# Float16 halves for every key block, rows of maxima by a transposition, and a written order of the heads' events

## The chip, the cores and the metric

The kernel runs on one core of a Trainium2 chip. The metric is device microseconds of one execution of the whole program: attention over 16 heads, a dense two-layer mixture, and a routed mixture of eight experts. The kernel before takes 713.42 us (median of three runs, 712.31 to 713.80).

In what follows PE is TensorE, ACT is ScalarE, DVE is VectorE, POOL is GpSimd and SP is SyncE. SBUF is the on-chip memory that all engines read, PSUM the one that PE writes its products to.

## The reference, cut to what matters

Attention compares only queries and keys whose random projections have the same six sign bits; all others are masked.

```python
q_bits = (einsum('bhsd,dk->bhsk', q, proj) > 0); k_bits = ...   # 6 bits a token
mask   = q_bucket[..., :, None] == k_bucket[..., None, :]
scores = where(mask, q @ k.T / sqrt(D), -1e9)                   # B=2, H=8, S=768, D=64
attn   = exp(scores - max(scores)); attn /= sum(attn) + 1e-9
x      = (attn @ v) as (1536, 512)
x      = (s * relu(x @ w_in)**2 + b) @ w_out                    # first mixture, d_ff 2048
e      = argmax(x @ w_gate + modality_bias[id])                 # second mixture, 8 experts
out    = gate * (relu(x @ w1[e]) @ w2[e])
```

A query whose bucket holds no key at all has a row of equal scores, so its result is the mean of all values. The kernel handles this with flags: a flag of such a query multiplies the sum of all values.

## The kernel before, in words

**Heads.** Two heads that share a batch entry make a pair (NP = 8 pairs). A head has 768 queries and 768 keys, in NB = 6 blocks of 128. Per pair, q and k come by transfer, are transposed on PE (`trans`, line 219), split into a high and a low part by ACT (line 227) and DVE (line 229), and copied into operand tiles Q1, K1, Q2, K2 by transfers on SP (`asm`); `bits` (line 286) makes the bucket bits.

**Maxima.** For each block of queries `maxp` multiplies Q1 by K1 (line 425) and DVE takes the row maximum from PSUM (line 428). When a head's six blocks are through, `mops` (lines 436 to 441) makes on DVE the shifted maximum in two bfloat16 parts, and the flags. `mrow` turns these columns into rows on PE with an identity: heads 0 to 3 by six products of a padded tile MD (line 447) and one of MP (line 448), after which ACT writes two rows of Q1 directly (line 450) and the flags (line 452); heads 4 to 15 by one product of MP (line 461), an ACT copy (line 464), an ACT copy of the flags NM (line 465) and two transfers on SP into Q1 (line 468). So the maximum is subtracted within the score product itself.

**Scores and values.** `st` computes a block of keys against all queries (line 477, four products into two PSUM banks), ACT takes the exponent into e (line 480), ACT rounds e to float16 eh (line 487), and POOL makes the rest el = e - eh (line 490). There are five buffers each for eh and el, four for e, and three score tiles of two PSUM banks. `avs` multiplies e by the values in two groups of three queries: with halves, three stationary eh blocks with two products each (high and low values VX) and three el blocks with one (line 501, `mm`). The constant NH = 5 says that only the first five blocks of a head are so treated, four for pair 7; the other blocks are multiplied in float32 (tile VW, no eh and no el). The last block's `avs` also multiplies the flags NM by the value sums VS. `fin` normalizes on DVE.

**Value sums and scales.** The values are scaled by a power of two taken from their mean size (`vabs`, `vred`, `vscale0` to `vscale2`), for three groups of pairs: 0, 1 to 3, 4 to 7. `vsums` (lines 388 to 394) makes the sums of all values of each head in parts on 12 partitions, in vb. `vsel` (line 399) spreads them for one pair on POOL into VS. `vxs` (line 405) scales the values, `vx` rounds them (line 412) and `vxl` makes the low part (line 416).

**Order.** Each engine takes its instructions in the order in which the program issues them. `program` lists the steps of all these functions as events; the part of a function up to a `yield` is one event. An event stands at 10 g + priority, with g the number of the key block in time (6 h + j); a step is named like `st:3,2/1`. The table MOVED gives 80 or so events another place. The events are sorted and issued. Work of the first mixture (`w_a`, `w_b`, `lead_k`, at g from 71 on) stands among the last heads. Behind the heads `Moe.program` issues the two mixtures, each in an order of its own.

Of the kernel before, what the change touches and what calls it, by code (L numbers as in the profile page):

```python
# [18 lines left out]
S = 768  # L19
# [9 lines left out]
NH = 5  # L29
XN = [[f"x{g}{i}" for i in "hl"] for g in range(3)]  # L30
MOVED = {
# [16 lines left out]
}  # L48
# [12 lines left out]
class Attn:  # L61
    def __init__(self, ctx, natctx, hlctx, qkctx, qkctx2, tc, psS, psA, ident, identb, q, k, v, proj, xt, x1, x2):
# [31 lines left out]
        self.MP = [c.tile([128, 128], BF16, name=f"MP{i}") for i in range(2)]  # L94
        self.MD = [t[1 + i][:, 1408:1408 + HALF].bitcast(BF16).rearrange("p (j q) -> p j q", j=NB) for i in range(2)]
        self.WD = [w[:, 128 * i:128 * i + 128] for i in range(2)]
        self.VX = [c.tile([128, 2, NH, 130], F16, name=f"VX{i}") for i in range(2)]
        self.VW = [c.tile([128, 2, 1 + i, 66], F32, name=f"VW{i}") for i in range(2)]
        self.VS = [c.tile([128, NB, 2, 66], F16, name=f"VS{i}") for i in range(2)]
        self.NM = [c.tile([128, 128], F16, name=f"NM{i}") for i in range(3)]  # L100
# [54 lines left out]
    def setup2b(self):  # L155
        nc = self.nc
        for i in range(2):
            nc.gpsimd.memset(self.MP[i], 0.0)
            nc.gpsimd.memset(self.MD[i], 0.0)
            nc.gpsimd.memset(self.VX[i][:, :, :, 64:65], 1.0)  # L160
            nc.gpsimd.memset(self.VW[i][:, :, :, 64:65], 1.0)
            nc.gpsimd.memset(self.vb[i][:, :, 65:66], 0.0)
            nc.gpsimd.memset(self.VS[i], 0.0)
        for i in range(3):
            nc.gpsimd.memset(self.NM[i], 0.0)
# [18 lines left out]
    def vmask(self):  # L184
        nc = self.nc
        idv = self.ident[0:12, 0:12].rearrange("p (c j) -> p c j", c=2)
        nc.vector.tensor_reduce(out=self.msk[:, 0:2], in_=idv, axis=AX.X, op=ALU.add, negate=True)
        nc.vector.tensor_tensor(out=self.msk[:, 2:8], in0=idv[:, 0], in1=idv[:, 1], op=ALU.add)
# [157 lines left out]
    def nh(self, p):  # L346
        return NH - (p == self.NP - 1)

# [25 lines left out]
    def vscale2(self, i):  # L374
        o = 256 * (i == 0)
        ps = self.vtile(i)[:, o:o + 3]
        self.nc.tensor.matmul(out=ps, lhsT=self.one[0:1], rhs=self.vsr[0:1, 0:3])
        yield
        self.nc.vector.tensor_copy(self.sc[i], ps)

    def vsums(self, lo, hi):
        nc, V = self.nc, self.nc.vector
        a, n = lo // 4, 2 * (hi - lo)
        hs = slice(2 * lo % 8, 2 * lo % 8 + n)
        cs = slice(hs.start * D, hs.stop * D)
        r0, p1, vb, src = self.vr0[:, cs], self.vp1[:, cs], self.vb[a], self.vtile(self.group(lo))[0:12, cs]
        sc = self.sc[self.group(lo)][0:12, 2:3]
# [3 lines left out]
        V.scalar_tensor_tensor(out=vb[:, hs, 0:D], in0=p1.rearrange("p (h d) -> p h d", h=n), scalar=self.msk[:, 1:2],  # L391
                               in1=r0.rearrange("p (h d) -> p h d", h=n), op0=ALU.mult, op1=ALU.add)
        V.tensor_scalar(out=vb[:, hs, D:D + 1], in0=self.msk[:, 0:1].unsqueeze(1).to_broadcast([12, n, 1]),
                        scalar1=-S * CSH * 2.0 ** -15, scalar2=None, op0=ALU.mult)

    def vsel(self, p):
        sh = [12, NB, 132]
        h = 2 * p % 8
        self.nc.gpsimd.tensor_tensor(out=self.VS[p % 2][0:12].rearrange("p j h d -> p j (h d)"),
                                     in0=self.vb[p // 4][:, h:h + 2].rearrange("p h d -> p (h d)").unsqueeze(1).to_broadcast(sh),  # L400
                                     in1=self.msk[:, 2:8].unsqueeze(2).to_broadcast(sh), op=ALU.mult)

    def vxs(self, p):
        vn = self.vn[p]
        self.nc.gpsimd.tensor_scalar(out=vn, in0=vn, scalar1=self.sc[self.group(p)][:, 0:1], scalar2=1.0, op0=ALU.mult, op1=ALU.mult)
        yield
        n = self.nh(p)
        self.nc.gpsimd.tensor_copy(self.VW[p % 2][:, :, 0:NB - n, 0:D], vn[:, :, n:])

    def vx(self, p):  # L410
        n = self.nh(p)
        self.nc.scalar.activation(out=self.VX[p % 2][:, :, 0:n, 0:D], in_=self.vn[p][:, :, 0:n], func=ACTF.Copy)

    def vxl(self, p, hh):
# [1304 lines left out]
```

## Time and profile before

| | |
|---|---|
| median of three runs | 713.42 us (712.31 to 713.80) |
| the profiled execution | 712.21 us, span 710.3 us |
| PE, busy | 677.8 us (95%) |
| PE's weight loads, busy | 595.4 us (84%) |
| DVE, busy | 423.6 us (60%) |
| ACT, busy | 368.8 us (52%) |
| POOL, busy | 238.5 us (34%) |
| mean granted TensorE clock | 0.992 |

The span runs from the first to the last instruction. The heads take about the first 268 us, the first mixture stands up to about 500 us, the routed one behind it. Busy shares are over the whole span, so ACT and POOL, which do most of their work among the heads, look emptier than they are there. A row in the next section that begins with a time gives the start in us, the length in us, the engine, the line of the kernel, the operation, its tile and shape and the number of merged instructions. Since products are pipelined, the step from one start to the next tells what a group takes; its own length holds the latency of the last one too.

### The profile page before, as it was taken

To read this page: it belongs to the slowest core of one execution; us is meant where nothing else is said; L and a number is where in the kernel's file an instruction comes from. 1 tells how busy PE (TensorE), PEld (TensorE's weight loads), DVE (VectorE), ACT (ScalarE), POOL (GpSimd) and SP (SyncE) were. 2 spreads that over 40 slices of the span, in tenths; PEclk is the share of its full clock that TensorE was granted. 3 is DMA by queue.
4 is the path that set the end of the run, shared out by engine and by line. 5 is a ranking of instruction groups with operands and counts; after the bars stand their busy time and mean duration, and the time that the engine had idled before them with its cause. 6 is when DMAs were issued, how large, how long until landed. Compare 5 with 4: busy or idle time off the path is not lost.

```text
span 710.3 us, 12827 instructions
## 1 busy us (share of the span) xinstructions
PE 677.8 (95%) x5003; PEld 595.4 (84%) x5003; DVE 423.6 (60%) x813; ACT 368.8 (52%) x580; POOL 238.5 (34%) x264
## 2 busy tenths in 40 slices
PE   9898999999989899999999999999999999999992
PEld 6677889988977788788888888888889999999992
DVE  5857766767667768888883432245663675645311
ACT  5666887787768775556542232232452263444411
POOL 8586887787767730000000000200110504040102
PEclk9999999999999999999999999999999999999997
DMA  9589345635571222344310000011431356354101
GB/s 194 140 209 211 72 105 119 152 87 122 122 173 55 61 90 90 119 139 128 118 60 0 16 31 15 1 45 50 138 113 45 115 186 211 119 168 147 45 16 47
DMA packets 52998, 72.33 MB, mean 102 GB/s; under 512 B 30320, under 2 KB 30832, under 8 KB 52928
## 3 DMA queue, kind: packets, MB, share of 16 engines
q1 hardware_dynamic: 49808, 62.24, 32.8%
q0 software_dynamic: 2960, 9.18, 4.0%
q8 instruction: 41, 0.67, 0.4%
q14 instruction: 29, 0.24, 0.1%
q10 hardware_dynamic: 160, 0.00, 0.0%
HBM read 46.31 MB, written 6.42 MB: 74 GB/s over the span
## 4 chain that ended last, share of the span: by engine, by line
PE 74%; ACT 8%; issue 7%; DVE 6%; POOL 2%; DMA 1%; SPq 0%; POOLq 0%; DVEq 0%; ACTq 0%
PE Y L1028 17%; PE H L970 16%; PE H L1345 8%; PE Y L1365 7%; PE Sst L477 7%; PE av L501 6%; ACT e L480 4%; PE Smaxp L425 3%; PE Sbits L286 2%; PE mlr L1058 1%; PE Strans L219 1%; ACT eh L487 1%; PE wps L269 1%; PE mxt L1332 1%; POOL out_dram L1419 1%
## 5 line engine op out<-in xcount | busy, mean ns | idle before, releaser
L490 POOL TENSOR_TENSOR el<-e,eh 128x768 f16<-128x768 f32 x78 | 128.5, 1651 | 55.4 <-ACT eh L487 40.9
L1028 PE MATMUL Y<-gh,W 128*128 128x512 f32 x384 | 128.8, 393 | 0.5 <-DVE sv L1038 0.5
L428 DVE TENSOR_REDUCE mx<-Smaxp 128x1 f32<-128x768 f32 x96 | 91.5, 983 | 42.9 <-PE Smaxp L425 42.8
L480 ACT ACTIVATE e<-Sst 128x768 f32<-128x768 f32 x96 | 77.3, 805 | 42.2 <-PE Sst L477 37.8
L477 PE MATMUL Sst<-Q,K 128*128 128x384 f32 x384 | 91.5, 360 | 6.7 <-DVE mx L428 2.9
L1028 PEld LDWEIGHTS Y<-gh,W 128*128 128x128 f32 x384 | 72.1, 188 | 15.6 <-DVE sv L1038 0.9
L1365 PE MATMUL Y<-hh,W 128*128 128x400 f32 x256 | 79.0, 353 | 0.0
L1028 PE MATMUL Y<-gl,W 128*128 128x512 f32 x192 | 74.8, 390 | 0.0
L983 DVE SCALAR_TENSOR_TENSOR r<-r,sb 128x512 f32<-128x512 f32 x46 | 35.8, 778 | 62.5 <-ACT r L982 62.3
L477 PEld LDWEIGHTS Sst<-Q,K 128*128 128x128 f32 x384 | 63.3, 190 | 11.1 <-ACT e L480 3.8
L487 ACT ACTIVATE eh<-e 128x768 f16<-128x768 f32 x78 | 65.8, 844 | 2.4
L982 ACT ACTIVATE r<-H 128x512 f32<-128x512 f32 x44 | 26.3, 597 | 78.1 <-PE H L970 78.1
L956 POOL IOTA ev<- 128x96 f32 x1 | 0.3, 299 | 190.5 <-PE H L970 190.5
L990 ACT ACTIVATE gh<-r,sb 128x512 fp32r<-128x512 f32 x46 | 33.2, 725 | 52.9 <-PE Y L1028 52.4
L425 PE MATMUL Smaxp<-K,Q 96*128 96x384 f32 x192 | 50.7, 350 | 5.6 <-ACT e L480 2.4
L991 DVE SCALAR_TENSOR_TENSOR gl<-r,sb,gh 128x512 fp32r<-128x512 f32 x46 | 34.4, 749 | 33.9 <-ACT gh L990 33.7
L501 PE MATMUL av<-VX,eh 128*128 128x65 f16 (+1 forms) x936 | 49.5, 194 | 0.0
L1252 DVE TENSOR_TENSOR W<-st,W 128x1024 fp32r<-128x1024 f32 x32 | 38.9, 1223 | 17.0 <-ACT W L1251 17.0
L501 PEld LDWEIGHTS <-eh 128*128 128x128 f16 x936 | 38.2, 98 | 12.9 <-issue 12.3
L1365 PEld LDWEIGHTS Y<-hh,W 128*128 128x128 f32 x256 | 47.6, 188 | 0.0
L1352 ACT ACTIVATE hh<-H 128x400 fp32r<-128x400 f32 x32 | 16.0, 501 | 55.1 <-PE Y L1365 46.1
L970 PE MATMUL H<-x1h,W 128*128 128x512 f32 x128 | 44.1, 396 | 0.0
(372 smaller groups left out, 1466.4 us busy)
## 6 DMA issues: line engine op xcount, KB each, us to landing
st<-in_moe_w_dram SPq DMA_DIRECT2D x32, 512.0 KB
sw<-in_moe_w_in_dram SPq DMA_DIRECT2D x16, 512.0 KB
sw<-in_moe_w_out_dram SPq DMA_DIRECT2D x16, 512.0 KB
Q<-qh SPq DMA_DIRECT2D x30, 192.0 KB
K<-kh SPq DMA_DIRECT2D x30, 192.0 KB
nq<-in_q_dram SPq DMA_DIRECT2D x16, 192.0 KB
nk<-in_k_dram SPq DMA_DIRECT2D x16, 192.0 KB
yd<-row SPq DMA_DIRECT2D x12, 256.0 KB
```

The lines of the kernel that those rows point to most:

```text
L425: nc.tensor.matmul(out=ps[:, a, 0:HALF], lhsT=self.Q1[i][0:96, j * 128:j * 128 + 128], rhs=self.K1[i][0:96, a * HALF:a * HALF + HALF])
L428: nc.vector.tensor_reduce(out=self.mx[h][:, j:j + 1], in_=ps[:, :, 0:HALF], axis=AX.XY, op=ALU.max)
L477: nc.tensor.matmul(out=ps[:, a, 0:HALF], lhsT=K[:, c], rhs=Q[:, a * HALF:a * HALF + HALF], start=(n == 0), stop=(n == 1))
L480: nc.scalar.activation(out=h2(e), in_=ps[:, :, 0:HALF], func=ACTF.Exp, scale=0.125)
L487: nc.scalar.activation(out=eh, in_=e, func=ACTF.Copy)
L490: nc.gpsimd.tensor_tensor(out=el, in0=e, in1=eh, op=ALU.subtract)
L501: mm = lambda q, n, e, v, start=False, stop=False: nc.tensor.matmul(out=av[:, q, 0:n], lhsT=e, rhs=v, start=start, stop=stop, skip_group_c ...
L970: self.nc.tensor.matmul(out=ps, lhsT=w[:, k, fs], rhs=x[:, k], start=(k == 0 and n == 0), stop=(k == 3 and n == 2))
L1028: nc.tensor.matmul(out=self.yp[d], lhsT=w[:, i, ds], rhs=x, start=(fc in (0, FA) and n == 0), stop=(fc in (FA - 1, 15) and n == 2))
L1252: nc.vector.tensor_tensor(out=lo[:, o], in0=d["st"], in1=f(hi[:, o]), op=ALU.subtract)
L1345: nc.tensor.matmul(out=ps, lhsT=w, rhs=xx[:, kd, 0:C], start=(n == 0), stop=(n == 11))
L1365: nc.tensor.matmul(out=self.yp[d][:, 0:C], lhsT=w, rhs=xx, start=(fc == 0 and n == 0), stop=(fc == 7 and n == 2))
```

## The change: what it does

- NH goes: all six blocks of every head are split into eh and el; VW and the float32 form of `avs` are gone, and VX holds six blocks.
- `mops` becomes two reductions: the maximum against a constant column, and a sum that gives each maximum twice, plainly and shifted. Only head 0 still uses MD. `mrow` of all other heads transposes these 12 columns in one float32 product. ACT copies the rows rounded, DVE makes the difference and (`flags`) the flags, straight from PSUM, and the two transfers on SP take every second row.
- `vsums` has one ACT copy instead of two; the count column of vb is written once at the start, by POOL. `vsel` is replaced by `vstore`: six small transfers on SP per group of pairs spread the sums into one tile VS for eight heads.
- MOVED is built from a list RUNS that places nearly every event of the heads, some 900, in runs of names between two positions. Counts of loads, score products, maxima and value products are as before.

```diff
-NH = 5
-MOVED = {
...
+RUNS = (
...
+    (60, 61, "st:0,4/2 vred:3/1 vabs:4/0 maxp:2,1/0 avs:0,2,1/0 vsums:0,1/1 avs:0,3,0/0 maxp:2,3/1 maxp:2,1/1 avs:0,3,1/0 mrow:1/3 "
+             "load_v:5/0 asm:1,k,(1,)/2 st:0,4/3 maxp:2,2/0"),
...
+    (560, 561, "bits:6/0 st:9,0/2 vstore:4,8/0 st:8,5/3 avs:8,2,0/0 fin:7/0 bits:6/1 st:9,1/2 maxp:11,2/0 vx:5/0 maxp:11,2/1"),
...
+MOVED = {n: lo + (hi - lo) * (i + 1) / (len(s.split()) + 1) for lo, hi, s in RUNS for i, n in enumerate(s.split())}
...
     def vsums(self, lo, hi):
...
-        nc.scalar.activation(out=r0, in_=src, func=ACTF.Copy, scale=sc)
-        nc.scalar.activation(out=p1, in_=src, func=ACTF.Copy, scale=sc)
+        nc.scalar.activation(out=vl, in_=src, func=ACTF.Copy, scale=self.msc[i])
         yield
...
-    def vsel(self, p):
...
+    def vstore(self, lo, hi):
+        hs = slice(2 * lo % 8, 2 * lo % 8 + 2 * (hi - lo))
+        for q in range(NB):
+            self.nc.sync.dma_start(out=self.VS[2 * q:2 * q + 2, q, hs], in_=self.vb[2 * q:2 * q + 2, hs])
...
     def mops(self, h):
...
+        V.tensor_reduce(out=mc[:, :, 0], in_=self.mx2[h % 3], axis=AX.X, op=ALU.max)
+        mx = self.mx[h] = self.sm.tile([128, NB, 2], F32, tag="mc", name="mc")
+        V.tensor_reduce(out=mx, in_=mc.unsqueeze(2).to_broadcast([128, NB, 2, 2]), axis=AX.X, op=ALU.add)
...
+    def flags(self, h, rows):
+        self.nc.vector.tensor_scalar(out=self.NM[h % 3], in0=rows, scalar1=-0.5 * PEN, scalar2=2.0 ** 15, op0=ALU.is_le, op1=ALU.mult)
 
     def mrow(self, h):
-        if h < 4:
+        if h == 0:
             yield from self.mrow0(h)
             return
...
-        nc.tensor.matmul(out=ps[:, 0:128], lhsT=MP, rhs=self.identb)
+        nc.tensor.matmul(out=ps, lhsT=self.mx.pop(h).rearrange("p j r -> p (j r)"), rhs=self.ident, is_transpose=True)
         yield
...
+        hl = [self.sm.tile([12, 128], F32R, tag=f"m{c}", name=f"m{c}", bufs=1) for c in range(2)]
+        nc.scalar.activation(out=hl[0], in_=ps, func=ACTF.Copy)
+        yield
+        nc.vector.tensor_tensor(out=hl[1], in0=ps, in1=f(hl[0]), op=ALU.subtract)
+        self.flags(h, ps)
         yield
...
     def st(self, h, j):
...
-        if j >= self.nh(h // 2):
-            self.E[h, j] = e
-            return
         yield
...
     def avs(self, h, j, t):
...
-        if j >= self.nh(p):
-            e = self.E[h, j]
-            for q in qs:
-                mm(q, 65, e[:, c(q)], self.VW[p % 2][:, hh, j - self.nh(p), 0:65])
-        else:
...
```

## Rows read from the trace of the kernel before

**Rows 1.** Stretches: from:to, length, busy us (instructions) by engine, clock, DMA share, GB/s.

```profile
20.00:80.00 60.00, 53.16 (x537) 44.74 (x535) 42.96 (x73) 43.33 (x66) 45.13 (x45) 0.97 0.72 163
80.00:180.00 100.00, 98.86 (x1165) 90.95 (x1160) 69.77 (x124) 79.88 (x117) 77.03 (x61) 1.00 0.53 117
180.00:260.00 80.00, 72.25 (x821) 63.24 (x820) 55.58 (x94) 61.16 (x92) 55.58 (x45) 1.00 0.38 98
268.00:680.00 412.00, 410.15 (x2224) 359.81 (x2224) 234.99 (x480) 164.56 (x271) 39.68 (x69) 1.00 0.28 91
```

**Rows 2.** Waits of PE: who waited for whom, total us, times, longest.

```profile
PE Sst L477 <- DVE mx L428: 2.9, 2, 2.4
...
PE Sst L477 <- ACT NM L465: 1.5, 1, 1.5
```

**Rows 3.** PE in order of time around the last block of a head and the next head.

```profile
151.28 0.78 PE L501 MATMUL av<-VW,e 128*128 128x65 f32 x6
151.89 0.25 PE L501 MATMUL av<-VS,NM 128*128 128x65 f16 x3
151.98 0.86 PE L501 MATMUL av<-VW,e 128*128 128x65 f32 x6
152.68 0.26 PE L501 MATMUL av<-VS,NM 128*128 128x65 f16 x3
...
153.91 0.36 PE L501 MATMUL av<-VX,eh 128*128 128x65 f16 x6
...
154.19 0.35 PE L501 MATMUL av<-VX,eh 128*128 128x65 f16 x6
...
154.47 0.22 PE L461 MATMUL Smrow<-identb,MP 128*128 128x128 bf16 x1
154.67 0.96 PE L477 MATMUL Sst<-Q,K 128*128 128x384 f32 x4
...
156.38 0.94 PE L477 MATMUL Sst<-Q,K 128*128 128x384 f32 x4
```

**Rows 4.** PE: the rows of maxima of head 2, and float32 transpositions elsewhere.

```profile
56.70 0.50 PE L447 MATMUL Smrow<-identb,tx0l 128*128 128x128 bf16 x6
57.04 0.22 PE L448 MATMUL Smrow<-identb,MP 128*128 128x128 bf16 x1
...
L365 PE MATMUL vps<-iw,vr 128*1 128x128 f32 x2 | 0.5, 272 | 0.0
```

**Rows 5.** ACT by line and shape: busy us, mean ns, idle before.

```profile
L480 ACT ACTIVATE e<-Sst 128x768 f32<-128x768 f32 x96 | 77.3, 805 | 42.2 <-PE Sst L477 37.8 <-PE Smaxp L425 2.3 <-POOL el L490 1.1
L487 ACT ACTIVATE eh<-e 128x768 f16<-128x768 f32 x78 | 65.8, 844 | 2.4
L450 ACT ACTIVATE Q<-Smrow 2x768 fp32r<-2x768 f32 x4 | 3.2, 804 | 5.5 <-PE Smrow L448 5.4
...
L465 ACT ACTIVATE NM<-Smrow 12x128 f16<-12x128 f32 x9 | 2.4, 266 | 0.2
```

**Rows 6.** POOL by line and shape, in the same form.

```profile
L490 POOL TENSOR_TENSOR el<-e,eh 128x768 f16<-128x768 f32 x78 | 128.5, 1651 | 55.4 <-ACT eh L487 40.9 <-issue 7.5 <-POOL el L490 2.7
...
L399 POOL TENSOR_TENSOR VS<-vb,msk 12x792 f16<-12x792 f16 x8 | 12.5, 1556 | 0.0
```

**Rows 7.** DVE by line and shape: the small operations of `mops`.

```profile
L436 DVE TENSOR_SCALAR mc<-mx 128x6 f32<-128x6 f32 x16 | 6.7, 417 | 0.1
L437 DVE TENSOR_SCALAR MP<-mx 128x12 bf16<-128x12 f32 x16 | 5.7, 357 | 0.0
...
L440 DVE CAST MP<-mc 128x6 bf16<-128x6 f32 x12 | 2.0, 170 | 0.0
```

**Rows 8.** POOL and DVE in order of time, from 59 to 63 us.

```profile
59.43 2.87 DVE L393 TENSOR_SCALAR vb<-msk 12x6 f16<-12x6 f32 x1
...
61.50 0.77 POOL L416 TENSOR_TENSOR VX<-tx0h,VX 128x320 f16<-128x320 f32 x1
```

**Rows 9.** The chain that ended last, in order of time: start, us, what.

```profile
38.75 2.33 DMA K<-aux
```

More of the change, by code (lines that the diff above doesn't have):

```diff
@@ L93, in __init__ @@
         self.Q1, self.K1, self.Q2, self.K2 = zip(*sets)
-        self.MP = [c.tile([128, 128], BF16, name=f"MP{i}") for i in range(2)]
-        self.MD = [t[1 + i][:, 1408:1408 + HALF].bitcast(BF16).rearrange("p (j q) -> p j q", j=NB) for i in range(2)]
+        self.MD = t[1][:, 1408:1408 + HALF].bitcast(BF16).rearrange("p (j q) -> p j q", j=NB)
         self.WD = [w[:, 128 * i:128 * i + 128] for i in range(2)]
[L97 to L100, printed above, removed]
+        self.VX = [c.tile([128, 2, NB, 130], F16, name=f"VX{i}") for i in range(2)]
+        self.NM = [c.tile([12, 128], F16, name=f"NM{i}") for i in range(3)]
         self.vsm = c.tile([128, 4, 2, D], F32, name="vsm")
@@ L104, in __init__ @@
         self.trow = t[2][0:1, 1024:1408].rearrange("p (a b) -> p a b", a=3)
-        self.vr0 = c.tile([12, n], F32, name="vr0")
-        self.vp1 = c.tile([12, n], F16, name="vp1")
+        self.vlo = c.tile([12, n], F16, name="vlo")
         self.junk = w[:, 512:512 + S]
-        self.vb = [c.tile([12, 8, 66], F16, name=f"vb{i}") for i in range(2)]
-        self.msk = c.tile([12, 8], F32, name="msk")
+        self.vb = c.tile([12, 8, 66], F16, name="vb")
+        self.VS = c.tile([12, NB, 8, 66], F16, name="VS")
+        self.msk = c.tile([12, 2], F32, name="msk")
+        self.msc = [c.tile([12, 1], F32, name=f"msc{i}") for i in range(3)]
+        self.mx2 = [c.tile([128, NB, 2], F32, name=f"mx{i}") for i in range(3)]
+        self.mc2 = [c.tile([128, NB, 2], F32, name=f"mc{i}") for i in range(2)]
         self.vm = c.tile([128, 8], F32, name="vm")
@@ L157, in setup2b @@
         for i in range(2):
-            nc.gpsimd.memset(self.MP[i], 0.0)
-            nc.gpsimd.memset(self.MD[i], 0.0)
             nc.gpsimd.memset(self.VX[i][:, :, :, 64:65], 1.0)
-            nc.gpsimd.memset(self.VW[i][:, :, :, 64:65], 1.0)
-            nc.gpsimd.memset(self.vb[i][:, :, 65:66], 0.0)
-            nc.gpsimd.memset(self.VS[i], 0.0)
         for i in range(3):
-            nc.gpsimd.memset(self.NM[i], 0.0)
+            nc.gpsimd.memset(self.mx2[i][:, :, 1], -0.5 * PEN)
+        for i in range(2):
+            nc.gpsimd.memset(self.mc2[i][:, :, 1], -8.0 * math.log(CSH))
+        nc.gpsimd.memset(self.MD, 0.0)
+        nc.gpsimd.memset(self.VS, 0.0)
+        nc.gpsimd.memset(self.vb, 0.0)
     def weights(self, W, o, a, heads):
@@ L184, in vmask @@
     def vmask(self):
[L185 to L188, printed above, removed]
+        V = self.nc.vector
+        V.tensor_reduce(out=self.msk, in_=self.ident[0:12, 0:12].rearrange("p (j c) -> p c j", c=2), axis=AX.X, op=ALU.add)
+        self.nc.gpsimd.tensor_scalar(out=self.vb[:, :, D:D + 1], in0=self.msk[:, 0:1].unsqueeze(1).to_broadcast([12, 8, 1]),
+                                     scalar1=S * CSH * 2.0 ** -15, scalar2=1.0, op0=ALU.mult, op1=ALU.mult)
     def ps(self, name):
@@ L427, in maxp @@
         yield
[L428 removed]
+        nc.vector.tensor_reduce(out=self.mx2[h % 3][:, j, 0:1], in_=ps[:, :, 0:HALF], axis=AX.XY, op=ALU.max)
     def mops(self, h):
[L431 to L441 removed]
+        V = self.nc.vector
+        mc = self.mc2[h % 2]
+        V.tensor_reduce(out=mc[:, :, 0], in_=self.mx2[h % 3], axis=AX.X, op=ALU.max)
+        mx = self.mx[h] = self.sm.tile([128, NB, 2], F32, tag="mc", name="mc")
+        V.tensor_reduce(out=mx, in_=mc.unsqueeze(2).to_broadcast([128, NB, 2, 2]), axis=AX.X, op=ALU.add)
+        if h == 0:
+            hi, lo = self.MD[:, :, 96], self.MD[:, :, 97]
+            P = self.nc.gpsimd
+            P.tensor_copy(hi, mx[:, :, 0])
+            P.tensor_tensor(out=lo, in0=mx[:, :, 0], in1=hi, op=ALU.subtract)
     def mrow0(self, h):
@@ L451, in mrow0 @@
         yield
-        nc.scalar.activation(out=self.NM[h % 3][0:12], in_=ps[0:12, 0, HALF:512], func=ACTF.Copy)
+        self.flags(h, ps[0:12, 0, HALF:512])
+    def flags(self, h, rows):
+        self.nc.vector.tensor_scalar(out=self.NM[h % 3], in0=rows, scalar1=-0.5 * PEN, scalar2=2.0 ** 15, op0=ALU.is_le, op1=ALU.mult)
     def mrow(self, h):
-        if h < 4:
+        if h == 0:
             yield from self.mrow0(h)
@@ L503, in avs @@
         c = lambda q: slice(q * 128, q * 128 + 128)
-        if j >= self.nh(p):
-            e = self.E[h, j]
-            for q in qs:
-                mm(q, 65, e[:, c(q)], self.VW[p % 2][:, hh, j - self.nh(p), 0:65])
-        else:
-            eh, el = self.E[h, j]
-            V = self.VX[p % 2][:, hh, j]
-            for q in qs:
-                mm(q, 65, eh[:, c(q)], V[:, 0:65], start=(j == 0 and q == 0))
-                mm(q, D, eh[:, c(q)], V[:, 66:66 + D])
-            for q in qs:
-                mm(q, 65, el[:, c(q)], V[:, 0:65])
+        eh, el = self.E[h, j]
+        V = self.VX[p % 2][:, hh, j]
+        for q in qs:
+            mm(q, 65, eh[:, c(q)], V[:, 0:65], start=(j == 0 and q == 0))
+            mm(q, D, eh[:, c(q)], V[:, 66:66 + D])
+        for q in qs:
+            mm(q, 65, el[:, c(q)], V[:, 0:65])
         if j == NB - 1:
             for q in qs:
-                mm(q, 65, self.NM[h % 3], self.VS[p % 2][:, q, hh, 0:65], stop=True)
+                mm(q, 65, self.NM[h % 3], self.VS[:, q, h % 8, 0:65], stop=True)
     def fin(self, h):
@@ L658, in program @@
         at(1, 6, self.vsums, 0, 1)
+        at(1, 7, self.vstore, 0, 1)
         for hh in range(2):
```

60 lines of the change are left out of this document (15 added, 45 removed), and 252 rows, old and new, of tables (MOVED, RUNS).

## The prediction

> **What bounds the kernel now.** I read the table of stretches first, then who TensorE waited for, then TensorE's own order of time around a sixth key block, and last the groups of the three engines that feed it. The stretches [rows 1] show TensorE (PE) busy 53.16 of 60 us, 98.86 of 100 and 72.25 of 80 between 20 and 260 us, where the heads run, and 410.15 of 412 us from 268 to 680 us, where the two mixtures run. So the mixtures are PE work from end to end; the change does not touch them, and whatever the heads save moves them forward as a block. Inside the heads PE is the fullest engine of every stretch: over 20 to 260 us it has 224.3 us of work and 15.7 us idle (6.8 + 1.1 + 7.8), while ScalarE (ACT) has 184.4 us, VectorE (DVE) 168.3 us and GpSimd (POOL) 177.7 us of 240. The middle stretch is bound by PE alone; the two outer ones by PE and by waits in turns. Those waits [rows 2] are short and have many owners: the largest is PE's score product waiting 2.9 us for a maximum on DVE, 2.4 us of it in one piece, and another of 1.5 us is for a flag copy that line 465 makes on ACT.
>
> **The change part by part.** *Sixth key blocks in halves.* 18 blocks (one per head for pairs 0 to 6, two per head for pair 7) leave the float32 form. From start to next start, one float32 group of three queries takes 0.61 us (151.28 to 151.89) and the other 0.70 us (151.98 to 152.68); a float16 group of nine products takes 0.28 us twice (153.91 to 154.19 to 154.47) [rows 3]. A block is two groups: 1.31 against 0.56, a saving of 0.75 us of PE. 18 x 0.75 = 13.5 us.
>
> What that costs elsewhere: 18 more copies eh at 0.844 us on ACT (15.2 us) and 18 more differences el at 1.651 us on POOL (29.7 us) [rows 5, 6].
>
> *Rows of maxima.* Heads 1 to 3 lose six bfloat16 products each, 0.34 us by the start times (56.70 to 57.04): 1.0 us of PE in all [rows 4]. The one product left per head becomes a float32 transposition; such a row lasts 0.272 us, the bfloat16 one 0.22 us [rows 4]. These are latencies of pipelined work, so 16 heads cost between 0 and 16 x 0.05 = 0.8 us; I take 0.4, the middle. ACT loses three two-row copies of 0.804 us for three small ones of some 0.27, and 16 flag copies of 0.266 us (four of them on line 452, costed alike): -1.6 and -4.3 us [rows 5]. DVE loses four small operations per head (0.417, 0.357, 0.170 us and a difference that I cost like the third) and gains four: two reductions, the flags and the difference of lines hl. No row shows these four. The nearest are the 12- and 6-column rows [rows 7]: 64 operations at 0.17 us add 10.9 us, at 0.42 us 26.9 us, against 16 x 1.11 = 17.8 us removed; so DVE moves by -6.9 to +9.1 us. I take 0.17 each, the nearest in what they read (the transposed row lies in PSUM, a reduction has one input). Either end stays below PE's load.
>
> The wide row is that of line 393: six numbers on 12 partitions took 2.87 us, from 59.43 us on, with a maximum queued behind it, for which PE then waited the 2.4 us [rows 2, 8]. So small operations on DVE were at times held for over a microsecond. The Trainium skill (SBUF - State Buffer, section "Who interferes with whom") says that DVE and GpSimd hold a shared pair of ports exclusively, that tensor_scalar and cast can take it and a reduction or an operation with at most one SBUF input outside the two-port modes does not. This trace agrees: POOL ran without a gap until its row of 61.50 ended at 62.27, and line 393's operation ended at 62.30 [rows 8]. By that rule the four new operations would never be held and DVE would fall by the full 6.9 us in spite of POOL's extra 30 us. The sum is the same by the rule and by the worse bound of the rows, since PE covers both ends.
>
> For heads 1 to 3 the row now goes by ACT, DVE and a transfer into Q1, where ACT wrote it directly. A small transfer took 2.33 us in the chain of waits [rows 9]. Bounds for three heads: 0 (products of the head before cover it) to 3 x 2.33 = 7 us; in the new list trans, maxima and value products of the head before stand between, so I take 1 us in all. Behind the waiting pair of transfers on SP stand the q, k and value-sum transfers, wanted several microseconds later.
>
> *Value sums.* Eight POOL selections of 1.556 us go (12.5 us) [rows 6]; 18 small transfers on SP take their place, in three bursts of six. The third overwrites rows that head 7 still reads, so it holds SP until those products are done; behind it stand parts of q and k for heads 12 and later, wanted by products some heads away. Its result is due at the end of head 8, about four blocks later. Bounds: 0 to 2.33 us of PE per burst, so 7 us at worst; I take 0, because value products of five blocks lie between. The copies of the float32 value block vanish and the lower halves grow by a sixth: about even on POOL. Line 393 leaves DVE, and with it 2.4 us of the 2.9 us wait.
>
> *The order.* Nearly every event of the heads gets a place of its own. I followed both lists by the PE work between them: from a block's score product to its value products stood 4 to 8 us, now 6 to 14, mostly 8 to 12. So PE is asked for a value product later after its halves were started, which is what extra work on ACT and POOL needs; it costs buffers. Counted along the lists, at most 4 of the 5 eh/el pairs were out at once, mostly 3; now 4 are typical, and all 5 at 26 of 96 blocks. I put the order's own effect at 0, between -13 (every stretch as full as the middle one, 1.1% idle) and +20 (rival C).
>
> *Loads after it.* Over the same 240 us: PE 224.3 - 14.1 = 210.2, ACT 184.4 + 15.2 - 5.9 - some 1.6 (half of the value-sum copies) = about 192, POOL 177.7 + 29.7 - 12.5 = 195, DVE 161 to 173. PE remains the fullest by 15 us; that margin hides the added copies and differences. If it were gone, each block would cost what POOL takes over PE.
>
> *Waits.* Leaving: 2.4 us (line 393) and 1.5 us (flags off ACT) = 3.9 us [rows 2]. Late next there are the exponents that free PSUM, in rows of a few tenths. Coming: 1 us for heads 1 to 3 (above), and 1 us at the very end, where head 15's last block now runs exp, eh and el, 0.81 + 0.84 + 1.65 = 3.3 us [rows 5, 6], with about 2.3 us of value products in front; bounds 0 and 3.3.
>
> **The sum.** PE work -13.5 - 1.0 + 0.4 = -14.1; waits -3.9 + 1 + 1 = -1.9; together -16.0 us. The profiled execution took 712.21 us, 710.3 of it span: 712.2 - 16.0 = 696.2. The median of the runs is 713.42, 1.2 above the profiled one, so I add 1.2 and get 697.4, **697 us**.
>
> **The rivals.**
>
> *A. The order also fills the outer stretches.* For it: the doubled distance from score to value products, and a middle stretch that reaches 1.1% idle already. Against: in the late stretch the mixture's weights are decoded on ACT and DVE among the heads, and that work stays. With all idle at the middle's rate, 240 us keep 2.7 of 15.7: 712.2 - 14.1 - 13 = 685 (686 as a median); half way there, 691. I give it 689.
>
> *B. Saved only where PE alone binds.* In the outer stretches the float32 block may be where ACT and POOL caught up; there the shorter PE work turns into waiting for el. For it: in a plain block POOL's 1.65 us and ACT's 0.81 + 0.84 us are close to the 1.71 us from one score product to the next (154.67 to 156.38) [rows 3]. Against: a head has transpositions, bucket products and value flags besides, so on average PE has 15 us more than POOL. Heads 4 to 9 keep 6 x 0.75 = 4.5 us, the other 12 blocks' 9 us are lost: 697.4 + 9 = 706.
>
> *C. Slower: the five eh/el pairs run out.* With value products placed later, ACT must hold the copy eh until PE has finished with a pair; behind that copy on ACT stands the next exponent, which alone frees a score bank, and PE stops for want of a bank. Place: the 26 blocks where all five pairs are out. Price: up to one exponent and one copy, 0.81 + 0.84 us, each; the gain of 16.0 us is gone at 0.62 us a place, and at 0.75 us the time is 697.4 + 19.5 = 717. Against: the pair that is awaited was given back by products placed before the copy, so PE has mostly passed them.
>
> *D. The halves do not shorten PE,* because its rows' ends are modelled. Start to start differs by 0.33 and 0.42 us a group wherever I looked, so I leave it 0.02, at 711.
>
> **How the numbers follow.** Forecast 0.55 (own range 692 to 702), A 0.13, B 0.20, C 0.10, D 0.02. Differences under 0.2%, 1.4 us, can't be told from none in this kernel. Faster: forecast, A and nearly all of B and D, 0.86; same 0.04 (ends of B, D and C); slower 0.10, C. The range 686 to 712 reaches through A and B and leaves out C and the far side of A, some 0.16.
>
> **What would show it.** Right: no float32 rows at line 501's place, 1728 + 96 float16 products there; el 96 times; the first mixture product after the heads some 16 us before 268; PE idle of 20 to 260 about 13 us; no wait of PE for a flag copy on ACT. B: PE's work down by 14 us but its idle up by 7 or more, el or exponents named as releasers. C: ACT's eh waiting for PE's av, and score products waiting for exponents, a dozen times or more. Wrong altogether: a time above 712, or the stretch from the heads' end to the program's end changed by more than 2 us.

## The result and the profile after

The kernel after takes 695.18 us (median of 4 runs, 693.91 to 695.75) against 712.87 us before (712.16 to 713.80, 4 runs in turn with it): a ratio of 0.9754, 95% interval 0.9739 to 0.9770, some 17.5 us faster. The forecast was 697 us, inside a range of 686 to 712. The total came out; two of its terms did not, and they offset each other: the order of the events did much more than I gave it, and the flag products became dearer, which I had not seen at all. That the total lies within 2 us of the forecast is, in that, luck.

The same table of stretches as [rows 1], now of after; its last row runs to the first product of the mixture.

```profile
20.00:80.00 60.00, 56.83 (x598) 48.15 (x596) 44.82 (x83) 48.66 (x73) 53.84 (x51) 1.00 0.62 148
80.00:180.00 100.00, 100.00 (x1291) 90.25 (x1288) 71.78 (x128) 84.32 (x118) 87.45 (x68) 1.00 0.62 144
180.00:260.00 80.00, 74.31 (x862) 59.87 (x862) 59.19 (x102) 65.31 (x98) 54.74 (x38) 1.00 0.35 97
252.00:664.00 412.00, 409.34 (x2219) 359.30 (x2218) 233.34 (x477) 163.20 (x268) 40.89 (x69) 1.00 0.27 90
...
20.00:251.17 231.17, 222.31 (x2701) 190.91 (x2699) 169.17 (x298) 194.28 (x281) 196.02 (x155) 1.00 0.55 133
```

And the stretch of before that answers to its last row:

```profile
20.00:268.13 248.13, 231.82 (x2599) 205.86 (x2597) 172.45 (x295) 189.50 (x282) 179.40 (x150) 0.99 0.52 121
```

The reader is to see three things. The heads end at 251.17 instead of 268.13 us, 17.0 us earlier; from there to the end of the span it takes 442.7 us after and 442.2 before, so the whole gain is in the heads and moves the mixtures forward as a block. PE's work between 20 us and the heads' end fell by 9.5 us, and its idle time (length less busy) from 16.3 to 8.9 us. And the middle stretch has no idle time left: PE is busy 100.00 of 100 us.

How the gain divides into work and idle time depends on the cut at 20 us, since the new order moves work out of the first 20 us. From the span's start to the heads' end, before and then after:

```profile
0.00:268.13 268.13, 250.23 (x2681) 218.47 (x2682) 184.43 (x325) 199.65 (x301) 194.99 (x191) 0.99 0.55 127
```

```profile
0.00:251.17 251.17, 238.85 (x2771) 201.41 (x2772) 180.41 (x325) 204.41 (x301) 211.76 (x191) 1.00 0.57 137
```

So of the 17.0 us, 11.4 are less work of PE and 5.6 less idle time (17.9 to 12.3).

PE's waits after, as [rows 2]. The waits for line 393's operation and for a flag copy on ACT are gone; the largest owner now has 2.2 us, 1.4 of it in one piece.

```profile
PE av L710 <- POOL el L699: 2.2, 2, 1.4
PE Sst L689 <- DMA K<-kl: 1.4, 1, 1.4
...
PE Sst L689 <- ACT e L692: 1.0, 3, 0.5
```

The groups of after by line and shape, ACT and POOL as [rows 5, 6] and DVE as [rows 7]:

```profile
L696 ACT ACTIVATE eh<-e 128x768 f16<-128x768 f32 x96 | 79.6, 838 | 2.1 <-PE av L710 0.9
...
L699 POOL TENSOR_TENSOR el<-e,eh 128x768 f16<-128x768 f32 x96 | 157.0, 1653 | 31.7 <-ACT eh L696 20.6 <-issue 5.0 <-POOL el L699 2.8
...
L663 DVE TENSOR_SCALAR NM<-Smrow 12x128 f16<-12x128 f32 x13 | 3.5, 270 | 0.3 <-ACT Q L658 0.3
L676 DVE TENSOR_TENSOR m<-Smrow,m 12x128 fp32r<-12x128 f32 x12 | 3.3, 273 | 1.0 <-ACT m L674 0.8
L644 DVE TENSOR_REDUCE mc<-mc 128x12 f32<-128x24 f32 x16 | 2.8, 178 | 0.7
...
L642 DVE TENSOR_REDUCE mc<-mx 128x6 f32<-128x12 f32 x16 | 2.6, 160 | 0.3
```

All 96 blocks run eh and el. ACT waited only 0.9 us in all for PE to give back an eh buffer, so the slower rival (C, the five pairs run out) did not occur, although the list has all five out at 26 blocks.

The surprise stands in PE's order of time, at the last block of a head, as [rows 3]:

```profile
147.34 0.35 PE L710 MATMUL av<-VX,eh 128*128 128x65 f16 x6
147.53 0.26 PE L710 MATMUL av<-VX,el 128*128 128x65 f16 x3
147.72 0.26 PE L710 MATMUL av<-VS,NM 12*128 12x65 f16 x3
147.91 0.36 PE L710 MATMUL av<-VX,eh 128*128 128x65 f16 x6
```

In [rows 3] the step from the start of the flag products NM to the next row is 0.09 us (151.89 to 151.98). Here there is 0.19 us from el to NM and 0.19 us from NM on, though each row by itself lasts 0.26 us as before. What differs is the shape: the change cut NM and VS from 128 partitions to 12.

### The profile page after: what moved, and what is told of

Same layout as the page of the kernel before. It is cut to its first block, busy times and chain, and to the rows that moved or that the text cites. A ratio compares the mean times of both kernels' runs of the same rounds, so it can differ in the third digit from the quotient of the medians.

```text
span 693.9 us, 13097 instructions
## 1 busy us (share of the span) xinstructions
PE 666.3 (96%) x5093; PEld 578.4 (83%) x5093; DVE 418.9 (60%) x811; ACT 372.3 (54%) x579; POOL 256.5 (37%) x264
## 4 chain that ended last, share of the span: by engine, by line
PE 55%; issue 8%; DVE 4%; ACT 2%; POOL 2%; DMA 1%; POOLq 0%; ACTq 0%; DVEq 0%
PE Y L1234 18%; PE H L1176 17%; PE H L1551 6%; PE Y L1571 6%; PE mlr L1264 2%; PE av L710 1%; PE mxt L1538 1%; POOL out_dram L1625 1%; DMA out_dram<-orow,ix 1%; ACT e L692 1%; PE Sst L689 1%; POOL xg L1524 1%; PE Smaxp L634 1%; DVE W L1093 1%; PE mid L1490 0%
## 5 line engine op out<-in xcount | busy, mean ns | idle before, releaser
L699 POOL TENSOR_TENSOR el<-e,eh 128x768 f16<-128x768 f32 x96 | 157.0, 1653 | 31.7 <-ACT eh L696 20.6
L689 PE MATMUL Sst<-Q,K 128*128 128x384 f32 x384 | 87.7, 353 | 3.5 <-DMA K<-kl 1.4
L696 ACT ACTIVATE eh<-e 128x768 f16<-128x768 f32 x96 | 79.6, 838 | 2.1 <-PE av L710 0.9
L710 PE MATMUL av<-VX,eh 128*128 128x65 f16 (+1 forms) x1152 | 62.3, 194 | 0.0
L710 PEld LDWEIGHTS <-eh 128*128 128x128 f16 x1152 | 47.5, 98 | 15.8 <-issue 13.9
L634 PE MATMUL Smaxp<-K,Q 96*128 96x384 f32 x192 | 53.0, 363 | 2.3 <-DVE mx L637 1.2
L710 PE MATMUL av<-VX,el 128*128 128x65 f16 x576 | 48.4, 193 | 2.2 <-POOL el L699 2.2
L1625 POOL DMA_INDIRECT out_dram<-orow,ix x16 | 15.5, 966 | 84.7 <-ACT orow L1591 58.8
```

Source lines behind the costliest of these rows:

```text
L634: nc.tensor.matmul(out=ps[:, a, 0:HALF], lhsT=self.Q1[i][0:96, j * 128:j * 128 + 128], rhs=self.K1[i][0:96, a * HALF:a * HALF + HALF])
L689: nc.tensor.matmul(out=ps[:, a, 0:HALF], lhsT=K[:, c], rhs=Q[:, a * HALF:a * HALF + HALF], start=(n == 0), stop=(n == 1))
L696: nc.scalar.activation(out=eh, in_=e, func=ACTF.Copy)
L699: nc.gpsimd.tensor_tensor(out=el, in0=e, in1=eh, op=ALU.subtract)
L710: mm = lambda q, n, e, v, start=False, stop=False: nc.tensor.matmul(out=av[:, q, 0:n], lhsT=e, rhs=v, start=start, stop=stop, skip_group_c ...
```

## The experiments

All were timed in five rounds in turn with the kernel before; each ratio is to that kernel. e9 to e12 ran on one chip and share its runs of before, so their times can be set side by side.

**e1_pad: the flag products on 128 partitions again.** After, with one thing undone:

```diff
-        self.NM = [c.tile([12, 128], F16, name=f"NM{i}") for i in range(3)]
+        self.NM = [c.tile([128, 128], F16, name=f"NM{i}") for i in range(3)]
 ...
-        self.VS = c.tile([12, NB, 8, 66], F16, name="VS")
+        self.VS = c.tile([128, NB, 8, 66], F16, name="VS")
 ...
+        for i in range(3):
+            nc.gpsimd.memset(self.NM[i], 0.0)
 ...
```

> The changed kernel with the flags NM and the value sums VS on 128 partitions again (rows 12 to 127 zero), all else as changed; the output is the same. Theory P: in the changed kernel's trace the step from the last el group to the flag product (147.53 to 147.72) and from the flag product to the next group (147.72 to 147.91) take 0.19 us each, where the kernel before took 0.09 (151.89 to 151.98); a product with 12 rows costs 0.10 us at its start and 0.10 us at its end, 32 groups x 0.20 = 6.4 us of PE, which is why PE's work fell by 11.4 and not by 14.1 us. It expects 695.2 - 6.4 = 689 us, and the two steps back at 0.09 us. Rival: the 0.19 is only how the rows are modelled, or is hidden: 694.5 to 695.7 us, no change.

688.57 us, ratio 0.9661 (0.9632 to 0.9691), as theory P expected. PE's order of time in this kernel, at a head's last block:

```profile
146.84 0.26 PE L712 MATMUL av<-VX,el 128*128 128x65 f16 x3
146.93 0.25 PE L712 MATMUL av<-VS,NM 128*128 128x65 f16 x3
147.03 0.34 PE L712 MATMUL av<-VX,eh 128*128 128x65 f16 x6
```

The steps are back at 0.09 and 0.10 us. 0.10 us at either side of 32 groups makes 6.4 us; 6.6 us were measured. PE's weight loads (PEld), which bring an operand into the array before its product, show where the steps grow; after, then e1, at the same places:

```profile
147.72 0.14 PEld L710 LDWEIGHTS <-NM 12*128 12x128 f16 x3
```

```profile
146.91 0.16 PEld L712 LDWEIGHTS <-NM 128*128 128x128 f16 x3
```

In e1 the load for the flags begins 0.07 us after the start of the group before (146.84), in after 0.19 us (147.53). The load itself is no longer; it no longer runs as far ahead. PE between 20 us and the heads' end:

```profile
20.00:244.44 224.44, 215.00 (x2697) 187.13 (x2696) 168.25 (x296) 193.48 (x281) 196.00 (x155) 1.00 0.57 137
```

7.3 us less work than after (222.31), with idle time about the same (9.4 against 8.9): the cost was PE's own.

**e11_flags_32_rows and e12_flags_96_rows.** e1 with 32 and with 96 in place of 128.

> The changed kernel with flags and value sums on 32 partitions (rows 12 to 31 zero). Theory Q: what costs is a change between products on all 128 rows and products on fewer, whatever the number: 695.2 us as with 12, and the two steps at 0.19 us. Rival: what costs is a number of rows that does not fill a group of 32: 688.6 us as with 128, steps at 0.09 us.

> The same on 96 partitions, the number of rows that the maxima's products use, which in the traces follow a value product after 0.09 us. Theory Q (any change of the number of rows costs): 695.2 us. Rival (only few rows cost): 688.6 to 690 us.

32 rows: 695.53 us, 0.9774 (0.9757 to 0.9791). 96 rows: 688.39 us, 0.9667 (0.9653 to 0.9680). PE at the same place, e11 and then e12:

```profile
147.43 0.25 PE L712 MATMUL av<-VX,el 128*128 128x65 f16 x3
147.62 0.26 PE L712 MATMUL av<-VS,NM 32*128 32x65 f16 x3
147.81 0.36 PE L712 MATMUL av<-VX,eh 128*128 128x65 f16 x6
```

```profile
144.67 0.25 PE L712 MATMUL av<-VX,el 128*128 128x65 f16 x3
144.76 0.26 PE L712 MATMUL av<-VS,NM 96*128 96x65 f16 x3
144.85 0.35 PE L712 MATMUL av<-VX,eh 128*128 128x65 f16 x6
```

So 32 rows cost what 12 cost and 96 rows cost nothing. It is neither any change of the row count nor a count that isn't a multiple of 32. Where between 32 and 96 it turns was not run.

**e2_halves_old_order: the halves alone.** Before, with all six blocks in halves and nothing else (VW and its copies go with it):

```diff
 ...
     def nh(self, p):
-        return NH - (p == self.NP - 1)
+        return NB
 ...
```

> The kernel before with one part of the change alone: all six key blocks of every head in float16 halves; the order, the rows of maxima and the value sums as before. Theory W (PE's work decides): 18 x 0.75 = 13.5 us of PE work go, 712.9 - 13.5 = 699.4 us, PE idle among the heads unchanged at about 18 us. Theory O (the order decides): in the old order the value products follow 4 to 8 us behind the score products and PE then waits for el on POOL; a good part of the 13.5 us comes back as idle: 704 to 710 us, PE idle up by 5 or more, el and exponents named as releasers.

720.78 us, ratio 1.0117 (1.0083 to 1.0150): by that ratio 8.3 us slower. Both theories expected a gain; the idle time that theory O expected came, and was more than the gain. The stretch of the heads in this kernel:

```profile
20.00:277.00 257.00, 224.83 (x2701) 192.75 (x2699) 188.60 (x295) 205.23 (x300) 207.92 (x160) 0.97 0.51 116
```

PE's work fell (231.8 to 224.8 us), but its idle time went from 16.3 to 32.2 us, and DVE, whose instructions were not touched, had 16 us more. Three stretches at the lower clock (around 73 to 77, 101 to 107 and 234 to 238 us) are part of why PE's work fell by 7.0 and not by 13.5 us. Who PE waited for, and DVE's small operations (as [rows 7]):

```profile
PE Smaxp L420 <- DVE mx L423: 7.0, 5, 2.4
PE Smrow L456 <- DVE mx L423: 5.0, 4, 4.0
...
PE av L496 <- POOL el L485: 3.0, 4, 1.4
```

```profile
L431 DVE TENSOR_SCALAR mc<-mx 128x6 f32<-128x6 f32 x16 | 11.6, 727 | 0.1
...
L436 DVE TENSOR_TENSOR MP<-mc,MP 128x6 bf16<-128x6 f32 x12 | 8.9, 744 | 0.4
...
L435 DVE CAST MP<-mc 128x6 bf16<-128x6 f32 x12 | 6.0, 503 | 0.0
```

0.417 and 0.170 us in [rows 7] have become 0.727 and 0.503 us for the same instructions. So the largest owner is not el, as theory O had it, but the maxima on DVE: 12.0 us in these two rows; in before all waits for a maximum come to 4.1 us, 2.9 of them in [rows 2]. The longest wait, POOL, DVE and PE in order of time:

```profile
96.53 5.30 POOL L485 TENSOR_TENSOR el<-e,eh 128x768 f16<-128x768 f32 x3
96.63 1.57 DVE L436 TENSOR_TENSOR MP<-mc,MP 128x6 bf16<-128x6 f32 x1
...
98.13 2.20 DVE L389 SCALAR_TENSOR_TENSOR vb<-vp,msk,vr 12x512 f16<-12x512 f16 x1
...
100.26 1.60 DVE L391 TENSOR_SCALAR vb<-msk 12x8 f16<-12x8 f32 x1
101.77 1.80 DVE L423 TENSOR_REDUCE mx<-Smaxp 128x1 f32<-128x768 f32 x2
102.77 0.26 PE L456 MATMUL Smrow<-identb,MP 128*128 128x128 bf16 x1 [3.99 <-DVE mx L423]
```

POOL runs three differences back to back, from 96.53 to 101.83 us. In that time three operations of DVE take 5.4 us in a row, the last ending at 101.86; the maxima behind them start, and PE has stood for 3.99 us. The granted clock had gone down to 0.50, the lower level of 1.2 GHz, at about 101 us, while PE stood, and PE then ran at it for 4.6 us:

```profile
102.77:107.36 4.59, 4.59 (x30) 4.29 (x30) 1.76 (x2) 2.19 (x4) 1.03 (x1) 0.50 0.21 49
```

**e3_contents_old_order: everything but the order.** After, with the old table MOVED in place of RUNS and vmask a few places earlier, so that its columns exist when they are read.

> All contents of the changed kernel (halves, rows of maxima, value sums) in the order of the kernel before, except that the little mask of 12 partitions is made earlier, since the scales now read it. Theory W: work as in the changed kernel, so within 3 us of it, 695 to 698 us. Theory O: 702 to 710 us, the difference to the changed kernel lying in PE's idle time among the heads and not in its work.

723.17 us, ratio 1.0144 (1.0109 to 1.0180): all that the change puts in, issued in the old order, is 10 us slower than before by that ratio, and slower than either theory had it. The largest wait of PE in it:

```profile
PE Sst L465 <- DMA Q<-m: 10.3, 3, 6.4
```

Those are the rows of maxima of heads 1 to 3, which now go by transfer. Before the longest of them SP, which issues these transfers, was late:

```profile
43.93 1.49 SPq L456 DMA_DIRECT2D Q<-m x2
```

DVE was done with that row at 41.25; SP was issuing parts of q and k until 43.8, and PE's product started at 47.90.

**e5_old_order_direct_rows and e6_new_order_direct_rows: those rows written by ACT again.** The same edit in e3 and in after:

```diff
-        if h == 0:
+        if h < 4:
             hi, lo = self.MD[:, :, 96], self.MD[:, :, 97]
-            P = self.nc.gpsimd
-            P.tensor_copy(hi, mx[:, :, 0])
-            P.tensor_tensor(out=lo, in0=mx[:, :, 0], in1=hi, op=ALU.subtract)
+            self.nc.scalar.activation(out=hi, in_=mx[:, :, 0], func=ACTF.Copy)
+            V.tensor_tensor(out=lo, in0=mx[:, :, 0], in1=hi, op=ALU.subtract)
 ...
     def mrow(self, h):
-        if h == 0:
+        if h < 4:
```

> The kernel of e3 (all contents of the changed one in the old order), but heads 1 to 3 write their maxima into Q1 directly from PSUM on ACT, by six products of the tile MD, as the kernel before did; ACT rounds the high part into MD, DVE makes the low part. Theory H (what sank the halves in the old order are DVE's small operations, held by POOL's el: 16 us more of DVE in e2; and in e3 the 10.3 us for rows that come by transfer): with neither, the halves' PE work counts even in the old order: 723.2 - 10.3 - some 2 us of half clock = 711 us or less, down to 706. Rival O (the short way from score to value products sinks them in any case): 718 us or more, PE's waits moving to el and exponents.

> The changed kernel, heads 1 to 3 with direct rows as in e5. The prediction put +1 us of waits on the transfers of these rows and -1.0 us on the six products that they save. Theory H expects the new order to cover the transfers wholly, so only the three times six products and three wide ACT copies come back: 695.2 + 1 = 696 us, at most 697. Rival: if the transfers still cost as they did in e3, this kernel is 3 to 8 us faster than the changed one.

e5: 717.93 us, 1.0063 (1.0040 to 1.0085): far from theory H's 711 or less and at the edge of rival O's 718 or more. Of PE's waits 4.3 us are for exponents and 2.4 for el, as O had it, and 2.5 for the difference that this edit itself puts on DVE (under e9). e6: 697.67 us, 0.9789 (0.9763 to 0.9814), 2.5 us slower than after and just above theory H's 697. So direct rows gain 5 us in the old order and lose 2.5 us in the new one, where after's waits have no row for these transfers.

**e9_old_order_direct_rows_128: e5 without the dear flag products.** e5 with the edit of e1, to take both known costs out of the old order.

> The kernel of e5 (all contents in the old order, direct rows for heads 1 to 3) with the flags and value sums on 128 partitions, as in e1. The gain of e1, 6.6 us, should come back here as well, if it is PE's work: 717.9 - 6.6 = 711.3 us. Theory N (new order needed): halves, maxima without held operations and full rows together bring nothing in the old order, 710 to 713 us, so that the order accounts for the 22 us to e1. Rival: the old order can use the saving once DVE is free, 700 to 706 us.

711.41 us, ratio 0.9988 (0.9971 to 1.0005): no change, as theory N expected. Its heads:

```profile
20.00:268.98 248.98, 224.45 (x2708) 191.23 (x2706) 168.69 (x296) 200.62 (x285) 195.63 (x152) 0.99 0.52 121
```

DVE's work is back at 168.7 us and PE's work is 7.4 us below that of before, but its idle time is 24.5 us: the old order turns the saving into waiting even so. One small operation that is held is left, and it is the experiment's own: the difference that the edit of e5 puts on DVE, with both inputs in SBUF.

```profile
L426 DVE TENSOR_TENSOR tx0l<-mc,tx0l 128x6 bf16<-128x6 f32 x4 | 4.6, 1142 | 4.2 <-ACT tx0l L425 4.2
```

```profile
PE Smrow L432 <- DVE tx0l L426: 2.5, 1, 2.5
```

So 2.5 us of the idle time are not the old order's alone. The new order takes 688.39 us (e12, with the rows of heads 1 to 3 by transfer), 23.0 us less; by e6 about 2.5 us of this are the direct rows.

**e4_f32_sixth_new_order and e10_f32_sixth_new_order_128: the order without the halves.** After (e10: e1) with the sixth blocks in float32 as before; ACT still copies such a block, to a float32 buffer, and POOL makes no difference for it.

```diff
 ...
+        if j >= self.nh(h // 2):
+            self.E[h, j] = pr.bitcast(F32)
+            nc.scalar.activation(out=self.E[h, j], in_=e, func=ACTF.Copy)
+            return
 ...
+        if j >= self.nh(p):
+            e = self.E[h, j]
+            for q in qs:
+                mm(q, 65, e[:, c(q)], self.VW[p % 2][:, hh, j - self.nh(p), 0:65])
 ...
```

> The changed kernel with its new order, but the sixth blocks (two for pair 7) multiplied in float32 again; ACT copies the exponent into the pair's buffer in float32 where it made eh, so ACT's work is the same, and POOL makes no el for them (18 x 1.65 = 29.7 us less). Theory W: PE gains 18 x 0.75 = 13.5 us of work and nothing else is short: 695.2 + 13.5 = 708.7 us. Theory O (order first): the sixth block hardly matters once the order is there, since PE's idle time shrinks: 696 to 702 us.

> The kernel of e4 (new order, sixth blocks in float32, ACT copying in place of eh) with flags and value sums on 128 partitions. It splits the whole change into terms that add up. Expected: 705.1 - 6.5 = 698.6 us, so that order, maxima and sums together are worth 14 us against the kernel before, the halves in the new order another 10 us (to e1), and the 12 rows take 6.6 us back. Rival: with float32 blocks next to the flags the 12 rows cost less, 701 us or more, and the halves are worth the full 13.5.

e4: 705.11 us, 0.9896 (0.9864 to 0.9927), between its two theories. e10: 700.38 us, 0.9837 (0.9821 to 0.9853), between the 698.6 us expected and the rival's 701. The heads in e10, from 20 us and from the span's start, and then in e1 from the span's start:

```profile
20.00:255.22 235.22, 228.20 (x2593) 203.56 (x2592) 168.24 (x297) 193.15 (x281) 167.30 (x145) 1.00 0.54 130
...
0.00:255.22 255.22, 243.95 (x2663) 213.64 (x2664) 179.50 (x324) 203.27 (x301) 183.53 (x186) 1.00 0.56 134
```

```profile
0.00:244.44 244.44, 230.92 (x2772) 197.52 (x2772) 179.99 (x324) 203.73 (x301) 212.14 (x194) 1.00 0.59 140
```

Against before, from the span's start on, PE in e10 has 6.3 us less work and its idle time is 11.3 instead of 17.9 us (from 20 us on: 3.6 us less work, and 7.0 instead of 16.3 us idle). From e10 to e12 the halves bring 12.0 us of time; from e10 to e1 they take 13.0 us off PE's work and add 2.3 us to its idle time.

**e7_new_order_pool_selection: POOL's margin.** After with the eight selections of line 399 on POOL again, in place of the 18 transfers:

```diff
 ...
-            self.nc.sync.dma_start(out=self.VS[2 * q:2 * q + 2, q, hs], in_=self.vb[2 * q:2 * q + 2, hs])
+        self.nc.gpsimd.tensor_tensor(out=self.VS[:, :, 2 * (p % 2):2 * (p % 2) + 2].rearrange("p j h d -> p j (h d)"),
+                                     in0=self.vb[p // 4][:, h:h + 2].rearrange("p h d -> p (h d)").unsqueeze(1).to_broadcast(sh),
+                                     in1=self.msk6.unsqueeze(2).to_broadcast(sh), op=ALU.mult)
 ...
```

> The changed kernel with the spread of the value sums done by POOL again, eight operations of some 1.56 us at places of the list where their buffers are free, in place of the 18 small transfers. It asks how much room POOL has left: POOL has 196 us of work in the 231 us of the heads. Theory M (the margin hides it): 12.5 us more of POOL cost 0 to 1.5 us, 695.2 to 696.7. Rival B (POOL is by now the other bound): each operation delays el by 1.5 us and PE follows: 700 to 708 us.

695.20 us, ratio 0.9746 (0.9721 to 0.9771): the same as after, as theory M expected. In the new order 12.0 us more on POOL (eight selections of 1.50 us) cost nothing.

**e8_before_count_column_on_pool: line 393 alone.** Before, with that operation on POOL:

```diff
-        V.tensor_scalar(out=vb[:, hs, D:D + 1], ...
+        self.nc.gpsimd.tensor_scalar(out=vb[:, hs, D:D + 1], ...
```

> The kernel before with one edit: the count column of vb (line 393) is written by POOL, not by DVE. The prediction took 2.4 us for the wait of PE behind that operation's 2.87 us. Theory V: that wait goes, and with it the 3.4 us at half clock that follow it in the trace (1.7 us): 712.9 - 2.4 - 1.7 = 708.8 to 710.5 us. Rival: line 391 ahead of it is held by POOL's run of work in its place, and the time stays at 712 to 713.

710.10 us, ratio 0.9968 (0.9951 to 0.9985): 2.2 us faster, as theory V expected, and the wait of 2.4 us [rows 2] is gone from the list. In before that wait had a second price, on PE behind it:

```profile
62.38 0.97 PE L477 MATMUL Sst<-Q,K 128*128 128x384 f32 x4 [2.38 <-DVE mx L428]
...
64.56 1.63 PE L477 MATMUL Sst<-Q,K 128*128 128x384 f32 x4
```

```profile
63.80:67.20 3.40, 3.40 (x21) 3.16 (x20) 2.08 (x3) 2.17 (x4) 1.64 (x1) 0.52 0.98 199
```

For 3.4 us the granted clock was 0.52, nearly all of it at the lower level of 1.2 GHz, and the same four score products took 1.63 instead of 0.97 us; 3.4 x 0.48 is a loss of 1.6 us. e8 shows no such stretch there, but one near its heads' end, which may be why it gained no more than the wait.

## Why the prediction was right or wrong

Side by side on one chip: before 711.8, e10 700.4, e12 688.4, e11 695.5 us. That is -11.5 for the order with the rows of maxima and the value sums, -12.0 for the halves on top of them, +7.1 for flag products on few rows. After lies at e11's time.

**Halves, -13.5: right in size, in the new order.** 12.0 us of time measured (e10 to e12), and 13.0 us of PE's work (e10 to e1). The working by start times held: 0.28 us a group in [rows 3] and in after, no float32 rows, 1824 products, 96 el. The step behind it, "that margin hides the added copies and differences", came true: e7 puts another 12.0 us on POOL for nothing. But its reason, sums over 240 us, was too weak. By the same sums e2, which keeps POOL's selections, still has PE ahead of POOL, by 210.8 to 207.4 us, and is 8.3 us slower than before. Only 3.0 us of its waits are for el. What the sums left out is that POOL's added work held DVE's small operations, and 12.0 us of PE's waits are for the maxima behind them. e9 has POOL's load as I summed it (195.6 us), and nearly all of DVE's operations free, and in the old order is still no faster than before. What the halves alone are worth in the old order once DVE is free is not shown: no run has the change's other contents there without them.

**"I put the order's own effect at 0, between -13 ... and +20": the step that was mis-sized.** With the sixth blocks still in float32, order, maxima and value sums together bring 11.5 us, where my terms for the last two and the waits sum to -2.5 (-0.6 and -1.9). The runs don't part the order from those two; but e9 has all the contents in the old order, with full flag rows and direct rows for heads 1 to 3, and gains nothing, so their gain hangs on the order. In work and idle time, from the span's start to the heads' end of before and e10, it is 6.3 us less work, of which I had 0.6 and the stretch at the lower clock in before (e8) explains 1.6, and 6.6 us less idle time.

The distance from score to value products that I had counted (4 to 8 us, then 6 to 14) I used only to argue that nothing would be lost. Rival A had the idle time right in kind: in the outer stretches it fell, to 3.2 of 60 and 5.7 of 80 us where [rows 1] have 6.8 and 7.8, and over 20 to 260 us it is 8.9 where I wrote "about 13"; but in the first 20 us it rose, from 1.6 to 3.5 us. A's 689 us and the 688.6 us of e1, with 128 flag rows, agree by luck: A's sum needs some 10 us less idle time beside 14.1 us less work, and from before to e1 the heads have 4.4 us less idle time (17.9 to 13.5) and 19.3 us less work (250.2 to 230.9).

**Flag products: not in the sum at all.** I followed how NM and VS are filled, and took their 96 products over unpriced because their count and their columns stay. The row count was in the diff; +6.6 us (e1 to after).

**Rows of maxima.** Transfers for heads 1 to 3, 1 us within 0 to 7: no such wait in after, 10.3 us of waits in the old order (e3), above my upper bound. The bound was one transfer a head; the longest single wait was 6.4 us, for the whole way by ACT, DVE, SP's queue and the transfer. I had counted what stands behind this pair on SP, not what stands before it: 2.7 us of the way in e3.

**DVE's small operations.** I took 0.17 us for each of the four new ones: 0.16 and 0.18 for the reductions, 0.27 and 0.27 for the flags and the difference. DVE's work over the heads fell by 3.3 us, not 6.9. (By my own bound of +9.1 the upper end of "161 to 173" should have been 177.) "The sum is the same by the rule and by the worse bound of the rows, since PE covers both ends" was wrong as a statement: e2 has DVE's operations held, less work on DVE than PE has, and 12.0 us of PE's waits for maxima. The Trainium skill (SBUF — State Buffer, section "Who interferes with whom") draws the line between operations that can be held by POOL and those that can't. The runs agree with it: beside the added el of e2, tensor_scalar, cast and the difference of two SBUF inputs went to 0.73, 0.50 and 0.74 us, the difference of e9 took 1.14 us, and with the reductions and PSUM inputs of after, beside as many el, none is above 0.27 on average. So replacing them was no detail. That it is part of what lets the halves pay is likely by e2, but not shown: in the new order the old operations were not tried.

**Waits.** Line 393: 2.4 us predicted, 2.2 measured (e8). The flag copy on ACT: gone from the list. End of the heads: 1 us predicted, within 0 to 3.3; PE's row there is

```profile
250.22 0.27 PE L710 MATMUL av<-VX,el 128*128 128x65 f16 x3 [1.36 <-POOL el L699]
```

**Value sums, 0:** right; selections or transfers give one time (e7). **The mixtures, 0:** right, 442.2 and 442.7 us.

**What stays open:** why the new order needs so much less waiting. e9's largest single owner of a wait has 3.4 us of its 24.5 us idle, and the rest is in rows of about three microseconds or less. Beside e1 most owners shrink: exponents from 4.6 to 1.4 us, maxima from 2.3 to 0.5, ACT's work for the first mixture (PE's wait lH) from 3.1 to 0.8, aux transfers from 1.9 to nothing, el only from 3.4 to 2.5. So it is no single place, and which runs of names do it was not tried. Nor was PE's work in the heads the same for nearly the same products: e9 has 224.45 us and e1 215.00 from 20 us on. The 18 products for direct rows in e9 (1.0 us) and stretches at the lower clock (mean granted 0.99 against 1.00) account for only part of it.

## What to carry to other kernels

Price a saving on the fullest engine against the program's order: it counts only if the engines that pay for it deliver before that engine's list reaches the product, and if their added work holds up no third engine. Sums over a stretch show neither; e2 and e10 to e12 are the same exchange of products, at +8.3 and at -12.0 us, in two orders and with different small operations on DVE. When a diff changes the shape of an operand of TensorE, look at the step from start to start on both sides of the product, not at its count and columns: cutting unused rows cost 6.6 us here, and putting them back (e1, or 96 rows as in e12) gives the best version of this study, 688.4 to 688.6 us, which beats both kernels. Small operations on VectorE of the kinds that were held here (tensor_scalar, cast, two SBUF inputs) are, beside a busy GpSimd, to be costed by the longest row and not by the mean.

## What the runs showed of the hardware that was not expected

A float16 product of 65 columns on 12 or 32 rows between products on 128 rows costs 0.10 us more at its start and 0.10 us more behind it (steps of 0.19 against 0.09 us); on 96 rows it costs nothing. Its own row lasts 0.26 us in every case, so the cost shows only in the steps.

A wait of 2.4 us was followed by 3.4 us at a granted clock of 0.52 (before, in e8's section), and in one of 3.99 us the clock went down to 0.50 while PE still stood and kept PE there for 4.6 us (e2). After had no such stretch in its heads.
